# Start-up loads split over two DMA queues, one weighing operation for both planes, regrouped first norm and new orders in a two-layer spectral and MLP kernel

## The chip, the cores and the metric

The kernel runs on one core of one Trainium2 chip. The metric is device time in microseconds (us) of one execution; seven runs of the kernel before gave a median of 354.47 us (353.44 to 354.94). A core has TensorE (PE, its weight loads are PEld), VectorE (DVE), ScalarE (ACT), GpSimd (POOL) and SyncE (SP), each of which takes its instructions in the order in which they are written, and 16 DMA engines that serve all queues.

## The reference, cut to what matters

Two kinds of block alternate, A, B, A, B, on x of 2048 rows by 512, in bf16:

```
x = x + A(layernorm(x));  x = x + B(layernorm(x));  and once more

A(x):  y = irfft2(rfft2(x) * (w_r + i w_i))          # w_r, w_i are 2048 x 257
B(x):  h  = gelu(layernorm(x) @ w1)                  # 512 x 512
       hs = shift(h) @ w2                            # four column groups, shifted by +1, -1, +2, -2 rows
       x1 = x + hs
       return x1 + gelu(layernorm(x1) @ w3) @ w4     # 512 x 1792, 1792 x 512
```

Both pairs of blocks use the same weights.

## The kernel before, in words

Row s of x is kept as partition s // 16 and slot q = s % 16, so a slot is a tile of 128 x 512. The transforms are matmuls with tables made on the host. A pair of blocks is one call of `layer` (L455), and each letter of an order string (ORDER_0 for the start, ORDER_A and ORDER_B for the two calls, L747 to L787) calls one small function with an index; a digit behind a point chooses the PSUM bank, a last letter V or A chooses DVE or ACT. Nothing reorders the instructions afterwards: the order strings are the order on every engine.

The start, `first_front` (L403). For each slot q: `s` takes the sums of the norm (DVE bn_stats L257, or, for slots in ON_ACT, two passes on ACT, L319 and L270), `i` aggregates them on DVE (L286), `f` does the same for the slots of ACT on POOL (L325 to L327), `S` takes the root on ACT (L331) for a group of slots, `J` its reciprocal on DVE (L334), `Q` scales the table T by it (DVE L348, ACT L350), `O` does the matmuls of a pair of slots (L361, L363) with FILL small matmuls on zeros behind it (L243), and `G` copies the result into V (L149 on DVE, L151 on ACT). V holds all slots.

The layer. `d` (L476) multiplies V by the table FA, `t` copies to SBUF (TV), `q` (L500) multiplies by the table TL, `x` copies (X), `p` (`weigh`, L515) multiplies X by the weights W, one DVE operation for the real plane and one for the imaginary one, into PB; `b` (L524) multiplies PB by the table TR, `m` copies into hT. A unit u is one or two of the 16 frequency blocks, and `d`, `t`, `q`, `x`, `p` work by unit. `d` of any block reads all slots of V. `N` (L710) makes a negated copy of half of TR on DVE, which `b` reads. When all `m` are done, `D` (L540), `Y`, `P` (L552) transform back, `a` (L560) adds to x, `s`, `r`, `n` normalise (ACT L270, POOL L276 to L304, DVE L339 or ACT L341), and `T` (L579) transposes by DMA from SP's queue. Then come the MLP matmuls: `v` (L591), `h` its gelu, `u` (L607), `f` and `k`, `o`, `U`, `w` (L642), `g` its gelu, `W` (L655), `A` (L660). At the end of the first layer the start of the second one is mixed in: `B`, `j` (norm sums, L257 and L286), `S` (POOL, L293 and L294), `Q`, `O`, `G`; there `G` of the first five pairs copies the right half on ACT and folds the left half with it on DVE (`fold_V`, L385). `X` puts matmuls on zeros into a named bank. `z` loads the gelu table on ACT (L715), and `L` permutes W on DVE (L704, L705).

Loads (`load_all`, L154). SP's queue carries, in this order, x in eight DMAs, FA, half of TL, and W in 18 DMAs (L208 to L211), with halves of TL and TR between them, then G and Tinv. A DMA on ACT's queue loads T. The DMA of W fills only the even partitions; at the end of `first_front` POOL copies them to the odd ones in four DMAs (L213, one for each quarter of the blocks), each of which waits for its quarter of W, with `turn_TL` (L219, L220) ahead of the first two, which makes the second half of TL from the loaded one. Then `load_mlp` (L187) loads w1 to w4 from SP's queue behind a small DMA that waits for the last copy of W.

Of the kernel before, what the change touches and what calls it, by code (L numbers as in the profile page):

```python
# [16 lines left out]
P = 128  # L17
# [136 lines left out]
def load_all(K, A_x, A_w_r, A_w_i, B_w1, B_w2, B_w3, B_w4):  # L154
# [14 lines left out]
    table("FA", nc.sync)  # L169
    K.TL = K.const.tile([P, NB, 2, P], BF16, name="TL")  # L170
    K.TR = K.const.tile([P, 3, NH, 64], BF16, name="TR")
    load_TL = lambda sl: nc.sync.dma_start(K.TL[:, sl, 0], dram["TL"][:, sl])
    load_TL(slice(0, 8))
    K.W = K.const.tile([P, 2, NH, 257], BF16, name="W")
    K.later = []
    for lo in range(0, NH, 8):
        for pl, w in enumerate((A_w_r, A_w_i)):
            load_W(K, w, pl, lo, lo + 8)
        if lo == 8:
            load_TL(slice(8, 16))  # L180
        if lo in (0, 16):
            nc.sync.dma_start(K.TR[:, 0:2, lo:lo + 16], dram["TR"][:, :, lo:lo + 16])
    for k in ("G", "Tinv"):
        table(k, nc.sync)
    K.load_G2 = lambda: nc.sync.dma_start(K.G[:], dram["G2"])

    def load_mlp():  # L187
        gate2 = K.const.tile([1, 16], BF16, name="gate2")
        nc.sync.dma_start(gate2[:], K.W[1:2, 1, NH - 1, 1:17])
        for k, w, n, c in (("w1", B_w1, 4, D), ("w2", B_w2, 4, D), ("w3", B_w3, 4, FH), ("w4", B_w4, 14, D)):  # L190
            t = K.const.tile([P, n, c], BF16, name=k)
            nc.sync.dma_start(t[:], w.rearrange("(t p) n -> p t n", p=P))
            setattr(K, k, t)
# [8 lines left out]
def load_W(K, w, pl, lo, hi):  # L202


    v = w.rearrange("(m j) f -> m j f", j=64)
    j1 = max(lo, 1)
    fwd, rev = [K.W[2 * sg::4, pl] for sg in range(2)]
    K.nc.sync.dma_start(fwd[:, lo:hi], v[:, lo:hi])  # L208
    K.nc.sync.dma_start(rev[:, j1:hi], v[:, 65 - hi:65 - j1][:, ::-1])
    if lo == 0:  # L210
        K.nc.sync.dma_start(rev[:, 0], v[:, 32])  # L211
    if pl == 1:
        K.later.append(lambda: K.nc.gpsimd.dma_start(K.W[1::2, :, lo:hi], K.W[0::2, :, lo:hi]))  # L213


def turn_TL(K, sl):

    old, new = [K.TL[:, sl, k].rearrange("p b (c h) -> p b c h", h=2) for k in range(2)]
    K.nc.gpsimd.tensor_scalar(new[:, :, :, 0], old[:, :, :, 1], -1.0, None, op0=ALU.mult)  # L219
    K.nc.gpsimd.tensor_copy(new[:, :, :, 1], old[:, :, :, 0])  # L220
# [25 lines left out]
class Stats:  # L246
# [156 lines left out]
def first_front(K):  # L403
# [51 lines left out]
def layer(K, last):  # L455
# [5 lines left out]
    PB = [K.grp.tile([P, 7, 2, 2, 256], BF16, name="PB", tag="gT") for _ in range(2)]  # L461
    n_pab = [0]
# [27 lines left out]
    def over_q(u):  # L490
# [5 lines left out]
        for i, b in enumerate(bs):  # L496
            for t in range(2):
                for h in range(2):
                    r = slice(64 * h, 64 * h + 64)
                    nc.tensor.matmul(o[:, h, i * 256:(i + 1) * 256], lhsT=K.TL[r, b, t],  # L500
                                     rhs=TV[r, i, t * 256:(t + 1) * 256], start=(t == 0), stop=(t == 1))

    def take_q(u, eng):
        X[u] = K.stream.tile([P, 2, 512], BF16, name="X", bufs=2)
        copy(K, X[u][:, :, 0:256 * len(UNITS[u])], ps.pop(("q", u)), eng)

    def weigh(u):
        n = len(UNITS[u])
        x = X.pop(u)[:, :, 0:256 * n].rearrange("p h (n f) -> p h n f", f=256)
        pab[u] = []  # L510
        for pl in range(2):
            t = PB[n_pab[0] % 14 // 7][:, n_pab[0] % 7]
            n_pab[0] += 1
            w = K.W[:, pl, 2 * u:2 * u + 2 * n, 1:257].rearrange("p (n h) f -> p h n f", h=2)
            nc.vector.tensor_tensor(t[:, :, 0:n], x, w, op=ALU.mult)  # L515
# [221 lines left out]
FILL = {0: 4, 1: 3, 2: 3, 3: 3, 4: 3}  # L737
GROUPS = [[0, 2, 3, 4], [7, 8, 9, 10], [11, 12], [14, 15], [1, 5], [6, 13]]
ON_ACT = [1, 5, 6, 13]
FIRST = [[0, 2], [3, 4], [1, 5], [7, 8], [9, 10], [11, 12], [6, 13], [14], [15]]  # L740
# [7 lines left out]
s0 s2 s1 s3 i3 s5 f4 i0 i2 s4 i4 S0 s7 J0 Q0P s6 Q3V Q4V s8 s10 S4 J4 i7 O1 Q2A O0 s9 s13 Q1P i8 f5 i10 i9 Q5V s11 S1  # L748
G1A J1 Q9V Q10V Q8P S5 s12 G0A i11 i12 O2 S2 O4 J5 Q7P s15 J2 G2A s14 i14 i15 Q12V Q11P O3 G4A Q6P S3 G3V O5 Q13A J3
Q15V Q14P O6 G6V G5A O8 G8A O7 G7A  # L750
"""
ORDER_A = """
d1.5 t1V d0.6 t0A d2.2 N0 t2A q1.4 d4.6 x1V p1 d10.4 t10V q0.0 t4A x0A p0 q2.2 x2A d6.6 t6V q4.4 x4A p2 p4 N1 d12.0
q6.6 t12A b1.3 d8.4 x6A p6 m1A q10.0 x10A p10 b3.2 b0.7 t8A b2.6 d14.1 m3A m0V m2A b6.0 q8.4 x8A t14V q12.2 x12A b10.7
m6V b5.1 m5A b4.5 d15.0 t15A b11.2 p8 p12 b9.6 q14.3 m4V m10A q15.0 x14A p14 x15A b7.7 m7A b12.3 m9A b13.1 m12A p15
b14.0 m13A m11V b8.7 m8A m14V b15.5 m15A m15V D1.1 D0.5 z0 L13 Y1V Y0A D3.3 P2.0 a2 Y3A P3.7 a3 s2 P1.6 a1 P0.0 a0
D2.4 s3 Y2V s1 s0 D4.1 Y4A r0 P6.6 a6 s6 P7.3 a7 P5.4 P4.6 a5 P9.3 s7 a4 s5 s4 n2V n3V T1 D5.0 Y5A D7.4 Y7A n0V n1V T0
D6.6 P8.2 a9 a8 P11.5 r1 n7V Y6A s8 P10.0 n4A c1 s9 n6V a11 s11 n5V P14.1 P15.6 a10 T3 a15 s10 P13.4 a13 s15 a14 T2
s13 s14 r2 P12.5 a12 L9 n8V v0.2 n11V n10V s12 r3 v1.0 h1 n9V T4 h0 v3.5 v2.0 h3 u0.7 h2 n12V n15V L14 T5 c0 u2.1 n14A
f2 T7 n13V E2 L11 u3.4 f3 k3 u1.2 f0 v4.0 k0 k2 v5.6 f1 k1 R0 h5 E0 E3 T6 c2 v6.4 v7.2 h4 u5.7 h6 h7 E1 o1V c3 u6.6  # L760
o3V f5 u13.4 u15.0 o0A U0 o2V f6 f13 E6 u10.6 f15 E15 k6 k13 u7.3 f7 k7 u9.7 E7 u4.0 k5 E5 f4 k4 E4 u8.5 f8 U1 f10 k10
R1 w5.2 g5 w0.5 f9 o6V g0 u11.7 w1.0 g1 L7 k9 w2.5 g2 L10 E8 o4A w3.3 g3 k8 w4.1 E13 u12.6 f12 L5 g4 o7V w6.4 U3 E12
E10 g6 W1.0 L1 L12 W2.2 f11 E11 A2 u14.1 f14 E14 k12 o5A k11 E9 U2 w8.4 g8 w9.6 g9 w7.1 g7 w10.6 k14 g10 w11.4 g11
W0.6 R2 o10V k15 R3 w13.4 o9V A0 w12.2 W3.7 g12 g13 o14A W4.4 W7.1 A1 B1 j1 L6 A3 o13V o11A W6.3 A7 B7 B3 j3 A6 o8A B6
U4 U5 w15.1 g15 w17.6 w14.0 g17 g14 w19.6 g19 A4 o15A U7 B0 j0 L4 B2 w16.4 g16 B4 j4 j2 w18.6 g18 w20.4 W5.0 S0 Q1
o12V U6 g20 W8.4 j6 W10.7 w21.1 g21 Q2 A5 B5 A10 L8 A8 W9.6 B10 L2 Q3 L15 A9 w25.4 g25 w23.6 w24.1 j5 L3 g23 B8 O1.3
L0 W11.7 j8 w27.5 j7 S1 G1A G1V A11 w22.3 g27 Q6 j10 Q0 B11 B9 j9 Q7 g24 j11 S2 Q9 g22 w26.0 O3.4 G3A Q4 Q5 Q10 O2.6
G3V G2A g26 W12.3 Q8 A12 G2V B12 j12 W15.5 A15 B15 j15 O0.3 G0A G0V S15 W13.7 A13 B13 j13 W14.2 Q11 O5.5 G5A S12 Q12
S13 Q15 O15.7 A14 B14 j14 S14 Q13 O4.0 G4A G15V O6.3 G6A X4.0 Q14 O14.6 G14A X4.6 G4V G15A X8.2
"""  # L770
ORDER_B = """
d15.3 d1.6 t15A d4.0 t1V q1.2 x1A d8.4 t4V t8A q15.6 x15A p1 q4.2 d12.0 t12A x4V p15 p4 d10.6 t10A b1.3 q12.1 x12V m1A
p12 q8.4 x8A p8 d2.6 t2A d6.0 t6A d14.4 q10.6 x10A q2.2 x2A d0.5 b9.1 m9A t14V t0A p10 b12.6 m12V b4.4 m4A p2 b8.3 m8A
b13.0 q6.1 q0.6 m13A q14.4 x0V x6A p0 b5.3 m5A b15.0 b3.6 m3A b2.1 x14A b11.2 m11A m2A b0.6 p6 b7.7 p14 b10.4 m0A
b14.3 m7V m10A m15V m15A b6.5 m14V m6A D3.6 D2.0 Y2A D1.2 Y1A Y3V P6.4 a6 P4.5 a4 P5.6 s6 a5 s4 s5 P7.4 a7 s7 r1 D0.2
Y0V D5.6 Y5A P2.5 a2 P3.1 a3 P0.0 a0 P1.2 s2 a1 P11.4 s3 s0 s1 D4.5 r0 n5A P10.7 n7V D6.2 n6V Y6A a11 D7.0 s11 Y7A n4V
Y4V T3 P8.5 n0A a10 P13.6 n2V n3V s10 c1 a13 s13 P12.4 n1V a8 P9.2 a9 s8 P14.1 T2 P15.0 a15 v2.6 a12 a14 s9 r2 n9V
n10V T1 h2 n8V s12 s15 s14 r3 v3.2 T0 n11V h3 v1.6 v0.4 c0 h1 n14V h0 T5 u3.7 n13A u2.5 u0.0 f0 u1.1 f1 T4 v5.3 v4.1
n15A n12A f2 k1 E2 f3 E3 h5 u4.0 f4 k0 k3 T6 h4 k2 R0 T7 v6.3 h6 v7.1 h7 k4 E1 o1V u15.3 E4 o2V o3V U1 E0 c3 u13.5 f13
u14.6 f15 o0A u5.0 f14 u8.2 c2 f8 k8 u10.7 u12.6 f12 u9.2 E8 f9 k9 u6.5 f6 k15 E6 f5 E5 f10 u7.1 f7 U0 w4.2 k6 E7 g4  # L780
k7 k10 w0.6 w2.4 g2 u11.1 f11 E11 k13 E10 k5 R1 o4V g0 w5.2 g5 E15 w1.4 k11 w3.2 g1 R2 o6A o7V g3 o5A E9 U3 U2 w6.5 g6
E12 o11A W1.2 A1 W3.1 y1 E13 A3 y3 w12.2 g12 w9.6 o8A g9 w8.2 g8 w10.0 g10 E14 w7.4 g7 w11.2 g11 w13.0 g13 W4.3 o10A
# [35 lines left out]
```

## Time and profile before

| | |
|---|---|
| median of seven runs | 354.47 us |
| the profiled execution: its time, its span | 354.14 us, 352.2 us |
| granted TensorE clock, mean | 0.999 |
| busy share: PE, ACT, DVE, POOL | 97%, 57%, 53%, 20% |
| start, until the first `d` | 0 to 20.90 us |
| first layer: `d` to `b`; `D` to `P`; MLP | to 41.79; to 57.15; to 183.25 us |
| handover to the second layer, until its first `d` | 183.25 to 189.00 us |
| second layer: `d` to `b`; `D` to `P`; MLP | to 208.84; to 224.09; to 348.75 us |
| last addition and store | to 352.2 us |

The span is that of the profiled execution, from its first to its last instruction; about 2 us of its time lie outside of it. A row of a timeline gives start, duration, engine, line, operation, what is written and read, and in brackets the idle time ahead of it and who ended it. A PE that is shown as busy may still be waiting behind the end of its last matmul, which is modelled, so the starts of the matmuls tell more than the busy share.

### The profile page before, as it was taken

What the parts mean: (1) busy time and instruction counts of PE and PEld (TensorE: products, weight loads), DVE (VectorE), ACT (ScalarE), POOL (GpSimd) and SP (SyncE); (2) the same over time, 40 slices, a digit from 0 to 9 for tenths busy, and PEclk for the clock granted to TensorE, in tenths of its full rate; (3) what the DMA queues carried; (4) which work ended last, traced back from release to release, by engine and by line L of the source; (5) the groups of instructions that cost most, each with busy time, mean ns of one, the idle gap of its engine ahead of it and who ended that gap; (6) DMA issues with size and microseconds to landing.
All of it is one profiled execution on the core that took longest, in us unless ns stands there. A gap on an engine that the chain in (4) does not pass through costs nothing.

```text
span 352.2 us, 5586 instructions
## 1 busy us (share of the span) xinstructions
PE 340.9 (97%) x2124; PEld 188.7 (54%) x2124; DVE 184.9 (53%) x442; ACT 200.7 (57%) x355; POOL 68.8 (20%) x171
## 2 busy tenths in 40 slices
PE   8889899999999999999999999999999999999996
PEld 6667785444444444444557888544444444444442
DVE  5869989669270444176576979845732004001003
ACT  5989899585736406213416979976583660442400
POOL 1440037462030101001120004645050010000000
PEclk9999999999999999999999999999999999999999
DMA  7996926611030030300000000763003005101003
GB/s 234 274 331 228 376 72 120 119 36 26 1 61 0 0 61 18 72 0 2 1 2 0 2 2 2 121 106 64 12 7 85 0 0 106 45 0 47 0 30 104
DMA packets 47210, 24.35 MB, mean 69 GB/s; under 512 B 36816, under 2 KB 43984, under 8 KB 47184
## 3 DMA queue, kind: packets, MB, share of 16 engines
q1 hardware_dynamic: 46464, 21.84, 24.8%
q0 software_dynamic: 576, 2.11, 1.5%
q8 instruction: 16, 0.26, 0.3%
q14 instruction: 10, 0.08, 0.1%
q10 hardware_dynamic: 144, 0.07, 0.1%
HBM read 11.41 MB, written 2.10 MB: 38 GB/s over the span
## 4 chain that ended last, share of the span: by engine, by line
PE 79%; ACT 6%; DMA 6%; issue 3%; DVE 3%; SPq 1%; POOL 1%; POOLq 0%; DVEq 0%; ACTq 0%
PE ps L655 27%; PE ps L642 27%; PE ps L591 8%; PE ps L607 8%; ACT hT L151 2%; PE ps L476 2%; DMA xT<-xn 2%; PE ps L540 2%; DVE x_state L560 2%; ACT xn L270 1%; DMA x_state<-in_A_x_dram 1%; PE ps L500 1%; DMA W<-W 1%; DMA W<-in_A_w_i_dram 1%; PE ps L524 1%
## 5 line engine op out<-in xcount | busy, mean ns | idle before, releaser
L649 ACT ACTIVATE gT<-ps 128x1024 bf16<-128x1024 f32 x56 | 56.6, 1024 | 84.1 <-PE ps L642 81.0
L642 PE MATMUL ps<-xT,w 128*128 128x512 bf16 x448 | 99.3, 379 | 0.0
L655 PE MATMUL ps<-w,gT 128*128 128x512 bf16 x448 | 99.0, 379 | 0.0
L660 DVE TENSOR_TENSOR x_state<-ps,x_state 128x512 bf16<-128x512 f32 x32 | 21.5, 689 | 111.7 <-PE ps L655 111.7
L642 PEld LDWEIGHTS <-w 128*128 128x128 bf16 x448 | 43.8, 98 | 52.9
L655 PEld LDWEIGHTS <-gT 128*128 128x128 bf16 x448 | 43.8, 98 | 52.1
L615 DVE SCALAR_TENSOR_TENSOR xn<-xn,ln_c,ps 128x512 bf16<-128x512 bf16 x32 | 23.2, 745 | 18.5 <-PE ps L607 16.1
L270 ACT ACTIVATE junk<-xn 128x512 bf16<-128x512 bf16 x32 | 19.9, 624 | 16.8 <-DVE xn L615 16.8
L591 PE MATMUL ps<-xT,w 128*128 128x512 bf16 x128 | 28.4, 379 | 0.8 <-DMA xT<-xn 0.8
L607 PE MATMUL ps<-w,hT 128*128 128x512 bf16 x128 | 29.1, 379 | 0.0
L276 POOL TENSOR_SCALAR ln_mv<-ln_s 128x4 f32<-128x4 f32 x16 | 5.5, 346 | 91.2 <-DVE x_state L560 52.2
L560 DVE SCALAR_TENSOR_TENSOR x_state<-ps,x_state 128x512 bf16<-128x512 f32 x32 | 20.4, 683 | 2.6 <-PE ps L552 1.9
L515 DVE TENSOR_TENSOR PB<-X,W 128x1024 bf16<-128x1024 bf16 (+1 forms) x40 | 21.0, 581 | 0.1
L591 PEld LDWEIGHTS <-w 128*128 128x128 bf16 x128 | 12.4, 98 | 16.1 <-issue 1.5
L607 PEld LDWEIGHTS <-hT 128*128 128x128 bf16 x128 | 12.5, 98 | 15.1
L257 DVE BATCH_NORM_STATS2 ln_st<-x_state 128x6 f32<-128x512 bf16 x28 | 18.8, 686 | 3.5 <-DMA x_state<-in_A_x_dram 3.2
L270 ACT ACTIVATE xn<-x_state 128x512 bf16<-128x512 bf16 x32 | 19.7, 620 | 0.5 <-DVE x_state L560 0.2
L598 ACT ACTIVATE hT<-ps 128x512 bf16<-128x512 f32 x32 | 17.2, 598 | 1.6 <-PE ps L591 1.5
L540 PE MATMUL ps<-G,hT 128*128 128x256 bf16 x128 | 15.1, 273 | 2.1 <-DVE hT L149 1.2
L476 PE MATMUL ps<-FA,V 128*128 128x256 bf16 x128 | 16.1, 273 | 0.8 <-DMA W<-in_A_w_i_dram 0.8
L552 PE MATMUL ps<-Y,Tinv 128*128 128x256 bf16 x128 | 15.8, 272 | 0.7 <-DVE Y L149 0.5
L293 POOL TENSOR_SCALAR ln_ve<-ln_mv 128x4 f32<-128x4 f32 (+1 forms) x15 | 3.6, 239 | 63.7 <-DVE ln_mv L286 63.0
(78 smaller groups left out, 402.0 us busy)
## 6 DMA issues: line engine op xcount, KB each, us to landing
w<-in_B_w_dram SPq DMA_DIRECT2D x2, 1792.0 KB, 12.3
W<-W POOLq DMA_DIRECT2D x4, 514.0 KB, 4.7
x_state<-in_A_x_dram SPq DMA_DIRECT2D x8, 256.0 KB, 5.4
out_dram<-x_state SPq DMA_DIRECT2D x16, 128.0 KB, 1.9
TR<-tab_TR SPq DMA_DIRECT2D x2, 512.0 KB, 5.3
w<-in_B_w_dram SPq DMA_DIRECT2D x2, 512.0 KB, 4.5
W<-in_A_w_r_dram SPq DMA_DIRECT2D x7, 128.5 KB, 5.0
W<-in_A_w_i_dram SPq DMA_DIRECT2D x7, 128.5 KB, 4.5
```

The lines of the kernel that those rows point to most:

```text
L270: K.nc.scalar.activation(out, src, ACT.Square, bias=0.0, scale=D ** -0.5, accum_out=self.s[:, i, 1:2])
L476: nc.tensor.matmul(oi[:, 1 - h], rhs=K.FA[:, t, h], lhsT=V[:, 2 * t + h, 2 * b:2 * b + 2].rearrange("d b q c -> d (b q c)"), start=(t == 0 ...
L515: nc.vector.tensor_tensor(t[:, :, 0:n], x, w, op=ALU.mult)
L540: nc.tensor.matmul(o[:, i, e * 256:(e + 1) * 256], lhsT=M[:, F, e, 2 * m + i, :], rhs=K.G[:, F, e, :], start=(F == 0 and e == 0), stop=(F ...
L560: nc.vector.scalar_tensor_tensor(K.x[:, q, :], ps.pop(("P", q)), 1.0, K.x[:, q, :], op0=ALU.mult, op1=ALU.add, accum_out=ln[g].s[:, i, 0:1])
L591: nc.tensor.matmul(o[:, i], lhsT=K.w1[:, t, j * P:(j + 1) * P], rhs=xT[g][:, :, t, :], start=(t == 0), stop=(t == 3))
L607: nc.tensor.matmul(o, lhsT=K.hT[:, j, st:st + P], rhs=K.w2[:, j, :], start=(j == 0), stop=(j == 3))
L615: nc.vector.scalar_tensor_tensor(xn[:, q, :], xn[:, q, :], ln[q // 4].c[:, q % 4:q % 4 + 1], ps.pop(("u", n)), op0=ALU.mult, op1=ALU.add, ...
L642: nc.tensor.matmul(o[:, i], lhsT=K.w3[:, c, t * P:(t + 1) * P], rhs=xT3[g][:, :, c, :], start=(c == 0), stop=(c == 3))
L649: nc.scalar.activation(gT[g][:, 2 * j:2 * j + 2, :], ps.pop(("w", k)), ACT.Gelu_apprx_tanh, bias=0.0, scale=1.0)
L655: nc.tensor.matmul(o, lhsT=gT[g][:, t, i * P:(i + 1) * P], rhs=K.w4[:, t, :], start=(t == 0), stop=(t == 13))
L660: nc.vector.tensor_tensor(K.x[:, q, :], ps.pop(("W", n)), K.x[:, q, :], op=ALU.add)
```

## The change

- Loads. ACT's queue now also carries the two small DMAs of W's odd rows (`rev[:, 0]` before), behind T and ahead of ACT's first operation. SP's queue carries x and then only W. FA, TL, TR and the copies of W to the odd partitions go to POOL's queue, in `load_rest`, together with the two `turn_TL`, in the order of the diff; POOL takes it up after its last operation of the start (`f1`). G and Tinv go behind the small DMA that waits for the last copy of W.
- `weigh` is one DVE operation for both planes: X is stored as 2n blocks of 256 and read twice, with a step of zero over the planes, and W and PB are read and written as 2 x 2n x 256. Each of the two PB tiles has three places for units of two blocks and one for a unit of one block, so four units of one block share two places; in the order of the second layer p14 writes the place of unit 15 ahead of b15, which then reads p14's values.
- The first norm has five groups of slots instead of six, in the order of the slots, and ACT takes the sums of slots 1 and 5 alone, not of 1, 5, 6 and 13. `f` works by slot. FILL is 3, 3, 2, 2, 2 instead of 4, 3, 3, 3, 3.
- TL is stored with the two halves apart. `scaled_T` can work on POOL, which no order uses.
- All three orders are new.

```
+    for pl, v in enumerate(planes):
+        nc.scalar.dma_start(K.W[2::4, pl, 0], v[:, 32])
+    for lo in range(0, NH, 8):
+        for pl, v in enumerate(planes):
+            load_W(K, v, pl, lo, lo + 8)
...
+    def load_rest():
+        q = nc.gpsimd
+        load_TL = lambda k: q.dma_start(K.TL[:, 0, 8 * k:8 * k + 8], dram["TL"][:, 8 * k:8 * k + 8])
+        load_TR = lambda k: q.dma_start(K.TR[:, 0:2, 16 * k:16 * k + 16], dram["TR"][:, :, 16 * k:16 * k + 16])
+        double = lambda k: q.dma_start(K.W[1::2, :, 8 * k:8 * k + 8], K.W[0::2, :, 8 * k:8 * k + 8])
+        table("FA", q)
+        load_TL(0)
+        double(0)
+        turn_TL(K, slice(0, 8))
+        load_TL(1)
+        load_TR(0)
+        double(1)
+        turn_TL(K, slice(8, 16))
+        double(2)
+        double(3)
+        load_TR(1)
...
         nc.sync.dma_start(gate2[:], K.W[1:2, 1, NH - 1, 1:17])
+        for k in ("G", "Tinv"):
+            table(k, nc.sync)
...
-        for pl in range(2):
-            t = PB[n_pab[0] % 14 // 7][:, n_pab[0] % 7]
-            n_pab[0] += 1
-            w = K.W[:, pl, 2 * u:2 * u + 2 * n, 1:257].rearrange("p (n h) f -> p h n f", h=2)
-            nc.vector.tensor_tensor(t[:, :, 0:n], x, w, op=ALU.mult)
...
+        k = n_pab[n]
+        n_pab[n] += 1
+        if n == 2:
+            t = PB[k % 2][:, 2 * (k % 6 // 2):2 * (k % 6 // 2) + 2]
+        else:
+            t = PB[k % 2][:, 6].rearrange("p (l h) f -> p l h f", l=2)
+        pab[u] = t
+        nc.vector.tensor_tensor(t, X.pop(u)[:, 0:2 * n].unsqueeze(1).to_broadcast([P, 2, 2 * n, 256]),
+                                K.W[:, :, 2 * u:2 * u + 2 * n, 1:257], op=ALU.mult)
...
-FILL = {0: 4, 1: 3, 2: 3, 3: 3, 4: 3}
-GROUPS = [[0, 2, 3, 4], [7, 8, 9, 10], [11, 12], [14, 15], [1, 5], [6, 13]]
-ON_ACT = [1, 5, 6, 13]
+FILL = {0: 3, 1: 3, 2: 2, 3: 2, 4: 2}
+GROUPS = [[0, 1, 2, 3], [4, 5, 6, 7], [8, 9, 10, 11], [12, 13], [14, 15]]
+ON_ACT = [1, 5]
```

The orders, at the places of which the prediction speaks: the start; the beginning of the first layer; its end; the beginning of the second one.

```
-s0 s2 s1 s3 i3 s5 f4 i0 i2 s4 i4 S0 s7 J0 Q0P s6 Q3V Q4V s8 s10 S4 J4 i7 O1 Q2A O0 s9 s13 Q1P i8 f5 i10 i9 Q5V s11 S1
-G1A J1 Q9V Q10V Q8P S5 s12 G0A i11 i12 O2 S2 O4 J5 Q7P s15 J2 G2A s14 i14 i15 Q12V Q11P O3 G4A Q6P S3 G3V O5 Q13A J3
-Q15V Q14P O6 G6V G5A O8 G8A O7 G7A
+s0 i0 s3 s2 i2 i3 s4 s1 f0 S0 J0 Q2V Q3V O1 i4 Q1V s6 s7 i6 s5 Q0A i7 s11 G1A f1 s9 S1 J1 O0 s8 G0A Q6A s10 i9 Q7A i11
+i8 i10 s13 Q4A O3 s12 Q5A S2 J2 G3A Q8A i13 i12 S3 O2 Q10V Q11V O5 Q9A s15 s14 G2A J3 i15 i14 S4 Q12V G5A Q13V O4 J4
+Q14V Q15V O6 G6A O7 G4V O8 G8A G7V
...
-d1.5 t1V d0.6 t0A d2.2 N0 t2A q1.4 d4.6 x1V p1 d10.4 t10V q0.0 t4A x0A p0 q2.2 x2A d6.6 t6V q4.4 x4A p2 p4 N1 d12.0
+d1.7 t1V d2.0 N0 t2A q1.2 d0.6 t0A x1V p1 d4.4 t4A d10.0 t10V q0.2 x0A q2.6 x2A p0 d6.4 t6V q4.2 x4A d12.0 t12A q10.4
...
-S13 Q15 O15.7 A14 B14 j14 S14 Q13 O4.0 G4A G15V O6.3 G6A X4.0 Q14 O14.6 G14A X4.6 G4V G15A X8.2
+G5A Q15 O15.5 A14 O4.6 G4A G15A B14 j14 S14 Q13 O6.3 X4.0 G6A G15V Q14 O14.0 G14A X8.2 X4.6 G4V
...
-d15.3 d1.6 t15A d4.0 t1V q1.2 x1A d8.4 t4V t8A q15.6 x15A p1 q4.2 d12.0 t12A x4V p15 p4 d10.6 t10A b1.3 q12.1 x12V m1A
+d15.0 t15A d4.4 t4A d1.3 d8.6 t1V q1.0 x1A p1 t8A q4.4 x4V q15.2 x15A p15 d12.0 p4 d10.6 b1.3 t12A q12.4 t10A x12V p12
```

In the first order a letter P behind Q falls to ACT before the change.

## The prediction

> **What bounds the kernel now.** I read the stretches of time first (span, each engine's busy time and count, clock, DMA share, GB/s):
>
> ```profile
> 10.00:15.00 5.00, 4.01 (x34) 3.15 (x33) 4.23 (x16) 5.00 (x15) 3.08 (x6) 1.00 0.96 267
> 35.00:40.00 5.00, 5.00 (x83) 4.55 (x81) 5.00 (x11) 5.00 (x11) 0.00 (x0) 1.00 1.00 379
> 82.00:156.00 74.00, 74.00 (x345) 33.55 (x344) 33.02 (x75) 31.97 (x46) 8.32 (x20) 1.00 0.13 25
> 251.00:330.00 79.00, 79.00 (x367) 35.82 (x366) 14.36 (x33) 39.12 (x56) 7.52 (x18) 1.00 0.14 32
> ```
>
> From 57 to 183 us and from 224 to 349 us PE is never idle, and the change adds and takes no matmul there: new orders can gain nothing in these 251 us, only lose. In the start ACT (fourth time) is full from 10 us on, and the DMA engines too (0.96). In the first part of a layer, `d` to `b`, ACT and DVE are both full.
>
> Then the chain of waits, in order of time, at the handover to the second layer, with DVE's timeline of the same place:
>
> ```profile
> 186.08 1.57 ACT V L151 x2
> 187.65 0.04 issue
> 187.69 1.47 PE ps L243 x12
> 189.16 1.75 PE ps L476 x16
> ```
>
> ```profile
> 186.64 1.42 DVE L385 TENSOR_TENSOR V<-ps,right 128x256 bf16<-128x256 f32 x4 [0.28 <-PE ps L243]
> ```
>
> V is complete at 188.06 (the fold, 186.64 + 1.42), but the first `d` starts at 189.0, behind twelve matmuls on zeros. And the fold waited for PE L243: matmuls on zeros that go to the bank it reads. This wait is about to grow.
>
> Last, POOL's timeline, since the loads move there, and the groups of the weighing operation with one row of it in time:
>
> ```profile
> 12.54 1.66 POOL L219 TENSOR_SCALAR TL<-TL 128x512 bf16<-128x512 bf16 x1
> 14.11 0.77 POOL L220 COPY TL<-TL 128x512 bf16<-128x512 bf16 x1
> 14.79 0.87 POOL L213 DMA_DIRECT2D W<-W  x1
> 20.95 1.65 POOL L219 TENSOR_SCALAR TL<-TL 128x512 bf16<-128x512 bf16 x1 [5.29 <-DMA TL<-tab_TL]
> ```
>
> ```profile
> L515 DVE TENSOR_TENSOR PB<-X,W 128x1024 bf16<-128x1024 bf16 x24 | 15.2, 688 | 0.0
> L515 DVE TENSOR_TENSOR PB<-X,W 128x512 bf16<-128x512 bf16 x16 | 6.0, 420 | 0.1
> ```
>
> ```profile
> 30.82 2.50 DVE L515 TENSOR_TENSOR PB<-X,W 128x1024 bf16<-128x1024 bf16 x4
> ```
>
> In a row, four operations of 1024 take 2.50 us, 0.62 each, and (38.10, four in 1.44) those of 512 take 0.36.
>
> **Part by part.** Differences are after minus before.
>
> 1. *Start, -0.4.* ACT did the sums of four slots (3.87 to 5.20 for one, 1.3 us each) and does two: -2.7. It scales 7 slots, not 9 (0.4 each): -0.8. DVE takes two more bn_stats (0.66) and aggregations (0.1), +1.5, two more scalings (0.25), +0.5, and one of its copies has 512 columns instead of 1024, -0.55. Laying DVE's new order end to end from 3.87, with 0.66, 0.1, 0.17 (reciprocal), 0.25 and 1.2, and holding it only for the arrival of slots 2 to 5 (6.48 in the chain), the last copy ends at 20.0; ACT's end is 20.1. Before it was 20.85. The two small loads on ACT's queue (0.6 each, the rows of L211) push the table load from 1.12 to 2.3; it ends at 3.6, ahead of the first x at 3.87: nothing, 0.2 if not covered. Of the 0.75 only half reaches ACT: its first copy of TV was of one block (21.98) and is now of two, `t2`, behind 12 matmuls of 0.11: 20.1 + 1.3 + 0.2 = 21.6. From there to `D` ACT has the same copies as before (by letters: six `t`, nine `x`, eleven `m`), 18.6 us with 0.7 idle. So `D` comes 0.4 earlier.
>
> 2. *Tables on POOL's queue, 0, up to +3.* `f1` waits for ACT's sums of slot 5 (ends 8.0) and takes 0.7, as L325 to L327 did. FA and half of TL are issued by 10.1 (0.7 each, the rows of L213), the first copy of W by 12.5, when its quarter has landed (13.46 before; its four DMAs now stand right behind x). FA needs 6.5 us to land by its old row, 16 us, and is wanted at 20.1. The critical one is the first half of TR: it stands behind `turn_TL`, which waits for TL. With TL's old 6.9 us, 2.4 for `turn_TL`, 1.4 for two issues and TR's old 5.3, TR lands at 26.1; with T's unloaded 2.8 both times, at 19.5. The bytes wanted by then (x 2.1, W 2.1, FA, TL and TR 1.3, one copy 0.5: 6.0 MB) at the 300 GB/s of the stretches from 2 us on give 22, which I take. `N0` on DVE waits for it, and behind `N0` stand `x1` and `p1`; ACT misses `x1` only when `N0` ends after 23.3 (x1 0.7, `q0` 0.5 and ACT's copy is due at 24.65), that is, TR lands after 22.8. So 0 with a cover of 0.8, +3.0 at 26.1, and no gain from an earlier landing, because ACT bounds the part. The other half of TR (28 to 30) is due at `N1`, 31. G now waits for the last copy of W (27 to 29), lands 4.2 later, and is due at 41. [...]
>
> 3. *One weighing operation, 0 on the path.* From 512 to 1024 an operation grows by 0.26; one of 2048 is 0.62 + 2 x 0.26 = 1.14 against 2 x 0.62, one of 1024 0.62 against 2 x 0.36. Per layer, six and four: 6 x 0.10 + 4 x 0.10 = -1.0 on DVE. ACT covers it: DVE's first-layer part sums to 17.8 from 20.8, ending 38.6, against ACT's 41. The upper bound is the copy from PSUM (L149, 1.22 per 1024): 2.3 and 1.2, +9 per layer on DVE, then 26.7 against 18.6, and `D` 6 later in each layer. The nearest row is L515 itself, with the same W at its odd start, so 1.14. [...]
>
> 4. *`D` to `v`, first layer, +0.3.* The gelu table (1.28) leaves its idle place at 41.3 for the place ahead of the first `h`; there ACT has it done at +17.3 (from `D`), `h1` can start at +17.5: hidden, 1.3 if ACT runs late. DVE's new order reaches `n1`, the last input of the first transposes, at +10.95 (before 52.47 - 41.79 = 10.7), and n6 at +14.75 (before 56.0, +14.3). The transposes follow, so 0.1 of the 0.4 is left at `v`.
>
> 5. *MLP parts, 0.* PE is at its floor; `U1` to the first `w` keeps some 0.4 of cover in the new order. Bound 0 to +1.
>
> 6. *Handover, +0.75.* Up to `O14` the steps after the last `W` are the same (A14, B14, j14, S14, Q14): `O14` starts at 186.41. Then the new order has X8 and X4 and only behind them the fold G4V, and X4.6 writes bank 6, which the fold reads. So 186.41 + 0.44 + 12 x 0.109 + 0.1 = 188.25, fold 1.42, `d` at 189.75 against 189.0.
>
> 7. *Second layer, +0.8.* By letters ACT takes one 1024 `t` (0.95) and one 512 `x` (0.54) more and one `m` (0.54) less, +0.95, DVE gives up 2.1. ACT now has 17.5 us of copies and 1.6 idle, most of it around the first copies; the new order keeps some 1.1 (`x1` waits for `t1` on DVE): 0.65 + 18.4 + 1.1 - 19.8 = +0.35, taken as +0.5 with the half `m` at the end. `D` to `v`: the last input of the transposes at +11.35, before +11.04: +0.3.
>
> Tail: last `W`, addition, store as before.
>
> Sum: -0.4 + 0.3 + 0.75 + 0.8 = +1.45: 354.14 becomes 355.6. The profiled execution lies 0.33 under the median of 354.47, so I forecast **355.8**. About 0.2%, 0.7 us, is what a measurement of this kernel can tell from no change.
>
> **Rivals.**
> - *The gaps of ACT close* (the other side: faster). DVE is lighter by 1.0 in the first layer and 2.1 in the second, so what ACT waits for comes earlier. For it: ACT's copies are 18.6 and 18.4, PE's matmuls of the part only 18.1. Price: the first layer gains its 0.7 of idle and the full 0.75; the second ends at 0.65 + 18.4 + 0.3 - 19.8 = -0.45, and `D` to `v` loses nothing. -1.45 - 0.45 + 0.75 = -1.15, 353.3. It decides when ACT is idle for under 0.4 us between its first TV copy and `D`.
> - *TR is late*, +2 to +3 on top of the sum: 358 to 359. For it: `turn_TL` sat 5.29 us waiting for TL before; against it: SP's weights drain by then.
> [...]
> - *Little of it shows*: the handover costs 0.75 and the start gives it back; 354.5.
>
> **How the numbers follow.** Forecast 0.40, gaps close 0.27, TR late 0.17, little shows 0.12, rate lost 0.04. The low end takes in the closed gaps with 0.7 to spare, 352.6; the high end late TR, 359.0. Slower: most of forecast, TR and rate, 0.56; faster: most of the gaps' case, 0.24; within 0.2%: 0.20.
>
> **What would show it.** First `d` near 20.1; `N0` at 22 to 23, DVE idle ahead of it for TR; the weighing (L527 in the changed file) at 1.2 for 2048; `D` near 41.4; at the handover the fold behind twelve L243 and `d` 0.7 later after the last `W`; second `D` some 20.3 after `d`. Wrong if PE idles in an MLP part, or if `D` moves by more than 1.

## The result, and the profile after

The changed kernel takes **355.82 us** (median of 22 runs, 354.21 to 358.18) against 354.01 us before (56 runs, 353.05 to 354.96): ratio 1.005, 95% interval 1.0039 to 1.0061. It is slower by 1.8 us, and the forecast was 355.8. As the points below show, that number came out in part by luck, because errors of opposite sign cancelled. Nine of the 22 executions have a mean granted TensorE clock of 0.989 to 0.995 and a median of 356.37; the other thirteen (0.998 to 1.000) have one of 354.98; run 1 has the profile of one execution with such a clock, 0.50 in one stretch of it.

The profiled execution took 355.86 us with a span of 354.1. I cut both spans at the same landmarks, which are starts of matmuls. The third row has the kernel in which the two waits found below are gone (the experiment e4_both).

| us | start to first `d` | `d` to `D` | `D` to `v` | `v` to last W | last W to second `d` | `d` to `D` | `D` to `v` | `v` to the end | span |
|---|---|---|---|---|---|---|---|---|---|
| before | 20.90 | 20.89 | 15.36 | 126.10 | 5.75 | 19.84 | 15.25 | 128.11 | 352.2 |
| after | 19.59 | 23.24 | 15.24 | 126.28 | 6.10 | 20.46 | 14.85 | 128.34 | 354.1 |
| e4_both | 18.76 | 21.47 | 14.84 | 126.26 | 5.33 | 19.87 | 14.74 | 128.33 | 349.6 |

Two cells of the row after stand out: `d` to `D` of the first layer, +2.35, and the handover with the part behind it, +0.35 and +0.62.

The stretches of the kernel after (span, then the busy time and count of PE, PEld, DVE, ACT and POOL, granted clock, DMA share, GB/s) first show what has not changed, the MLP part of the first layer, and then the place of the first loss, with the same three microseconds of the kernel before below it:

```profile
82.00:156.00 74.00, 73.98 (x343) 33.40 (x342) 34.05 (x82) 34.56 (x50) 9.59 (x20) 1.00 0.18 28
```

```profile
23.00:26.00 3.00, 1.12 (x15) 0.77 (x14) 2.05 (x3) 1.22 (x2) 3.00 (x5) 1.00 0.45 184
```

```profile
23.00:26.00 3.00, 3.00 (x35) 2.28 (x32) 2.42 (x4) 3.00 (x4) 1.70 (x3) 1.00 1.04 362
```

From 23 to 26 us PE works for 1.12 us of 3 and ACT for 1.22; before, both were full there (3.00 and 3.00). The DMA engines aren't full either (0.45, where the kernel before has 1.04). The chain of waits of the kernel after, in order of time (start, duration, what), names what is waited for:

```profile
18.02 5.86 DMA TR<-tab_TR
...
23.91 0.04 DVE TR L722
...
24.85 0.68 DVE X L149
25.53 0.05 issue
25.57 0.83 PE ps L509 x12
```

L722 is `N0`. On DVE, `x1` (24.85) stands behind it, and PE's next matmuls on TV (25.57) behind `x1`. DVE's timeline gives the idle time (first the kernel after, then the kernel before, where `N0` waits for nothing), and POOL's shows why TR was asked for only at 18.02:

```profile
23.91 1.01 DVE L722 TENSOR_SCALAR TR<-TR 128x1024 bf16<-128x1024 bf16 x1 [2.96 <-DMA TR<-tab_TR]
```

```profile
22.24 0.64 DVE L710 TENSOR_SCALAR TR<-TR 128x1024 bf16<-128x1024 bf16 x1
```

```profile
14.14 0.62 POOL L183 DMA_DIRECT2D W<-W  x1 [4.16 <-DMA W<-in_A_w_i_dram]
15.13 1.66 POOL L228 TENSOR_SCALAR TL<-TL 128x512 bf16<-128x512 bf16 x1 [0.37 <-DMA TL<-tab_TL]
16.72 0.76 POOL L229 COPY TL<-TL 128x512 bf16<-128x512 bf16 x1
17.41 0.61 POOL L181 DMA_DIRECT2D TL<-tab_TL  x1
18.02 0.73 POOL L182 DMA_DIRECT2D TR<-tab_TR  x1
...
22.34 1.63 POOL L228 TENSOR_SCALAR TL<-TL 128x512 bf16<-128x512 bf16 x1 [2.96 <-DMA TL<-tab_TL]
...
25.86 0.73 POOL L182 DMA_DIRECT2D TR<-tab_TR  x1
```

The load of TR waits in POOL's order behind a copy of W, which itself waited 4.16 us for its quarter of W, and behind `turn_TL` (2.4 us with its copy). In the kernel before, SP issued it at 10.97. From issue to landing it took 5.86 us, hardly more than the 5.3 of the kernel before (median of its two halves): TR was late because it was asked for late.

The second place, in the chain and in DVE's timeline of the kernel after:

```profile
187.26 0.42 DVE V L149
187.68 0.21 DVE Tq L358
...
188.53 1.32 PE ps L252 x12
...
189.88 1.43 DVE V L395 x4
191.30 0.05 issue
191.35 1.70 PE ps L485 x14
```

```profile
189.88 1.42 DVE L395 TENSOR_TENSOR V<-ps,right 128x256 bf16<-128x256 f32 x4 [2.00 <-PE ps L252]
```

DVE is free at 187.88 and the fold waits 2.00 us for twelve matmuls on zeros, four of which go to the bank that it reads.

These four do more than hold the fold up. `X4.6` writes its zeros over the left half of the first of `O4`'s two slots ahead of the fold, which then takes zeros for it; in the kernel before `X4.0` does the same, as `O4` has bank 0 there. Both kernels leave that half of one slot out of the second layer. Where an expectation below calls V of `O4`'s pair "the computed one", no zeros are written there.

And the weighing, as groups of shapes of the kernel after (busy us, mean ns, idle time ahead):

```profile
L527 DVE TENSOR_TENSOR PB<-X,W 128x2048 bf16<-128x2048 bf16 x12 | 14.4, 1224 | 0.1
L527 DVE TENSOR_TENSOR PB<-X,W 128x1024 bf16<-128x1024 bf16 x8 | 5.5, 691 | 1.4 <-ACT X L151 1.3
```

### The profile page after: what moved, and what is told of

The parts are those of the page before. It is cut to its first block, busy times and chain, and to the rows that moved or that the text cites. A ratio compares the mean times of both kernels' runs of the same rounds, so it can differ in the third digit from the quotient of the medians.

```text
span 354.1 us, 5547 instructions
## 1 busy us (share of the span) xinstructions
PE 339.9 (96%) x2120; PEld 188.0 (53%) x2120; DVE 183.8 (52%) x431; ACT 197.0 (56%) x340; POOL 71.9 (20%) x176
## 4 chain that ended last, share of the span: by engine, by line
PE 83%; DMA 5%; ACT 5%; DVE 4%; issue 1%; POOL 1%; DVEq 0%; POOLq 0%; ACTq 0%
PE ps L654 27%; PE ps L667 27%; PE ps L603 8%; PE ps L619 8%; PE ps L552 3%; PE ps L485 3%; PE ps L564 2%; PE ps L509 2%; ACT hT L151 2%; DMA TR<-tab_TR 2%; DMA TL<-tab_TL 2%; PE ps L536 2%; ACT X L151 1%; DMA x_state<-in_A_x_dram 1%; DMA xT<-xn 1%
## 5 line engine op out<-in xcount | busy, mean ns | idle before, releaser
L610 ACT ACTIVATE hT<-ps 128x512 bf16<-128x512 f32 x32 | 18.1, 597 | 8.7 <-PE ps L603 8.6
L266 DVE BATCH_NORM_STATS2 ln_st<-x_state 128x6 f32<-128x512 bf16 x30 | 19.9, 682 | 4.1 <-DMA x_state<-in_A_x_dram 3.8
L619 PEld LDWEIGHTS <-hT 128*128 128x128 bf16 x128 | 12.5, 98 | 15.1
L527 DVE TENSOR_TENSOR PB<-X,W 128x2048 bf16<-128x2048 bf16 (+1 forms) x20 | 19.6, 1011 | 1.5 <-ACT X L151 1.3
L151 ACT ACTIVATE X<-ps 128x1024 bf16<-128x1024 f32 (+1 forms) x17 | 14.4, 885 | 3.2 <-PE ps L509 2.5
```

What stands on the lines that cost most here:

```text
L151: K.nc.scalar.activation(dst, src, ACT.Copy, bias=0.0, scale=1.0)
L619: nc.tensor.matmul(o, lhsT=K.hT[:, j, st:st + P], rhs=K.w2[:, j, :], start=(j == 0), stop=(j == 3))
```

## The experiments

My theory after the result: the loss is two waits, `N0` for TR and the fold for the matmuls on zeros, less what the start gained. The rival: the new orders cost it inside the layers, or the loads on POOL's queue do so as a whole. Each kernel was timed against the kernel before on the same chip; "before" was 353.77, 353.96 and 354.14 us in the three groups (runs 1 to 4, 5 to 8, 9 to 12). A difference between kernels of different groups carries these 0.2 to 0.4 us.

**1. The fold without its wait (e1_fill_bank).**

```
-... X8.2 X4.6 G4V
+... X8.2 X4.2 G4V
```

> The changed kernel with the last four matmuls on zeros of the handover sent to bank 2 instead of bank 6, which the fold G4V reads. In this kernel no zeros are written over the left half of O4's result ahead of its fold, so V of that pair of slots is the computed one. Theory (the loss is two waits: N0 for TR in the first layer, and the fold behind twelve matmuls on zeros at the handover): the fold no longer waits 2.00 us for PE but starts when O4 and G4's right half are there and DVE is free; the first `d` of the second layer comes at the end of the twelve matmuls or of the fold, 0.8 to 1.2 us earlier from the last W, and the time falls from 355.8 to about 354.8. Rival (the new orders and the weighing cost it inside the layers): the first `d` waits for another thing as long, and the time stays within 0.3 of 355.8.

Measured: 354.13 us (353.18 to 355.86), ratio to before 1.0011 (0.9993 to 1.0028). DVE's and then PE's timeline of this kernel:

```profile
187.86 0.42 DVE L149 CAST V<-ps 128x256 bf16<-128x256 f32 x1 [0.90 <-ACT V L151]
188.20 0.28 DVE L358 TENSOR_SCALAR Tq<-T,ln_r 128x256 bf16<-128x256 bf16 x1
188.39 1.41 DVE L395 TENSOR_TENSOR V<-ps,right 128x256 bf16<-128x256 f32 x4
```

```profile
188.96 1.47 PE L252 MATMUL ps<-zeros 128*128 128x256 bf16 x12
190.27 2.46 PE L485 MATMUL ps<-FA,V 128*128 128x256 bf16 x21
```

The fold runs right behind DVE's other work, with no bracket. From the last W to `d` it is 5.32 us instead of 6.10, and `d` to `D` 19.88 instead of 20.46: 1.36 in all, because in the kernel after the first 24 `d` also took 3.37 us instead of 2.78, while the rest of the fold came in. I had counted only the first part. The rival said 0.3 at most, and falls for this place.

This profiled execution (355.04 us, mean granted clock 0.994) shows one thing more. Its first layer's `d` to `D` took 25.02 us, longer than the 23.24 of the kernel after, although `N0` came at the same time (24.05): the first `d` was earlier (18.45), so PE idled longer. PE's timeline, first of the kernel after, then of this one, and a stretch of this one:

```profile
25.57 0.83 PE L509 MATMUL ps<-TV,TL 64*128 64x256 bf16 x12 [1.88 <-DVE X L149]
```

```profile
25.25 1.46 PE L509 MATMUL ps<-TV,TL 64*128 64x256 bf16 x12 [2.70 <-DVE X L149]
26.64 1.89 PE L485 MATMUL ps<-FA,V 128*128 128x256 bf16 x8
```

```profile
25.50:28.00 2.50, 2.50 (x19) 1.53 (x16) 2.20 (x3) 1.62 (x2) 0.86 (x2) 0.50 0.86 322
```

Behind 1.88 us of idling the granted clock stayed at 1.00. Behind 2.70 us it was 0.50 from 25.5 to 28.0, and the same twelve `q` took 1.46 instead of 0.83, eight `d` 1.89 instead of 1.05: 1.5 us on top of the wait. Four of the twelve executions of run 1 have a mean clock of 0.994 or 0.995; the median of the other eight is 353.60, 1.4 below the 354.98 of the kernel after with its clock kept, so the fold's 1.36 is found there too. That the nine executions of the kernel after with such a mean lost it at this place is likely but not shown, as none of them was profiled; and a low mean alone doesn't make an execution long, for three of the kernel before with 0.994 and 0.995 took 354.23 to 354.73.

**2. `N0` behind `t6V` (e2_n0_late).**

```
-d1.7 t1V d2.0 N0 t2A ... x2A p0 d6.4 t6V q4.2
+d1.7 t1V d2.0 t2A ... x2A p0 d6.4 t6V N0 q4.2
```

> The changed kernel with N0 moved in DVE's order from ahead of x1 to behind t6V, so that x1, p1, t10V, p0 and t6V no longer stand behind its wait for TR (23.9 us). Theory: PE's idle 1.88 us at 25.6 and ACT's 1.79 at 26.0 go, `d` to `D` of the first layer falls from 23.2 to about 21.0 to 21.4, and the time from 355.8 to about 353.8. If TR is late for the first b as well (its reader b2.7), at most 0.5 of it comes back. Rival: ACT, which has as many copies as before, is the bound of the part and N0's wait was beside it; the time falls by less than 0.5.

Measured: 353.14 us (352.69 to 353.82, and one of 356.98), ratio 0.9991 (0.9970 to 1.0011): 2.7 below the kernel after, and 1.9 below it where only executions that kept their clock are compared (353.07 and 354.98). DVE's timeline of this kernel, over the same stretch:

```profile
20.26 0.69 DVE L149 CAST X<-ps 128x512 bf16<-128x512 f32 x1 [0.56 <-PE ps L509]
20.98 0.69 DVE L527 TENSOR_TENSOR PB<-X,W 128x1024 bf16<-128x1024 bf16 x1
...
25.66 0.54 DVE L722 TENSOR_SCALAR TR<-TR 128x1024 bf16<-128x1024 bf16 x1
```

`x1` starts at 20.26 instead of 24.85, and `N0`, at 25.66, waits for nothing. TR was asked for at 17.62, hardly earlier than in the kernel after; what moved is its reader. But for one of twelve (356.98, mean clock 0.993) the executions also lie within 1.2 us, those of the kernel after within 4.

**3. TR's load earlier on POOL's queue (e3_tr_early).** `load_TR(0)` moves from behind `load_TL(1)` to ahead of `double(0)`.

> The changed kernel with the load of TR's first half issued on POOL's queue ahead of the first copy of W, at about 10 us instead of 18.0. Theory: at 5.9 us from issue to landing TR is there at 16 to 18, N0 does not wait, and the time falls by about 2, to 353.8, as if N0 were moved; N0 takes 0.43 to 1.0 us. What may eat some of it: 512 KB come 8 us earlier into the stretch in which the DMA engines are full with x and W, so W's first quarter, its copy, and p1 come later; each us of that which DVE or ACT sees costs as much. Rival (the loads on POOL's queue as a whole take what the change loses): the first `d` or p1 comes later by as much as N0 comes earlier, and the time stays within 0.5 of 355.8.

Measured: 355.39 us (353.58 to 357.65), ratio 1.0051 (1.0024 to 1.0078). The median is that of the rival, the profiled run (354.04) that of the theory. In it, `N0` doesn't wait, but the next table does, a little:

```profile
20.71 0.41 DVE L722 TENSOR_SCALAR TR<-TR 128x1024 bf16<-128x1024 bf16 x1
...
31.70 0.43 DVE L722 TENSOR_SCALAR TR<-TR 128x1024 bf16<-128x1024 bf16 x1 [0.67 <-DMA TR<-tab_TR]
```

The copy of W was issued at 15.06 and the second half of TR at 26.55, both later than in the kernel after (14.14, 25.86). What the longer executions waited for isn't in this profile. The four longest (356.14 to 357.65) have a mean granted clock of 0.994 or 0.995, the other six (353.58 to 355.52) 0.997 to 1.000, so in those four PE may have idled as long as in the profiles of runs 1 and 10 (2.70 and 3.91 us), which is not shown; run 10 shows such a wait for a near relation.

**4. Both (e4_both).** The edits of 1 and 2.

> The first two changes together: N0 behind t6V, and the last four matmuls on zeros to bank 2. As in the first, V of O4's pair of slots is the computed one. Theory: the two waits are in different parts and add up, 355.8 - 2.0 - 0.9 = about 352.9, some 1.1 faster than the kernel before; this is then what the earlier start, the lighter weighing and the new orders are worth without the two waits. Rival: it stays at or above the kernel before (354.0), and the new orders themselves cost time.

Measured: 352.20 us (351.41 to 352.31, and one of 357.10), ratio 0.9951 (0.9933 to 0.9969). Less the two waits, the change is faster than the kernel before by 1.6 us (353.77 in this group); the fold's part of it, against run 2, is 0.94. The execution of 357.10 has a mean clock of 0.990.

**5. The kernel before with fewer matmuls on zeros (e5_before_fill).** `X4.6` and `X8.2` go from its handover.

> The kernel before without the twelve last matmuls on zeros of its handover (X4.6 and X8.2). Theory: in the kernel before, V was complete at 188.06 and the first `d` stood behind these twelve at 189.0; without them `d` comes 0.7 to 0.9 after... that is, 0.7 to 0.9 earlier, and the time falls from 354.0 to about 353.2. The twelve are then what the handover already paid before the change. Rival: without them PE gets a lower granted clock for the first matmuls behind the gap, and the time stays at 354.0 or grows.

Measured: 352.96 us (351.99 to 353.73), ratio 0.9969 (0.9956 to 0.9982). PE's timeline there:

```profile
188.24 1.92 PE L476 MATMUL ps<-FA,V 128*128 128x256 bf16 x16 [0.96 <-ACT V L151]
```

From the last W to `d` it is 4.73 us instead of 5.75; the sixteen `d` run at their usual pace (1.92 us, as in the first layer), the granted clock is 1.0, and the parts behind are the same to 0.1 (19.85, 15.30). So these matmuls kept nothing up here that the run shows; they cost 1.0 in the kernel before too.

**6. Two weighing operations (e6_two_ops),** in the kernel of run 4.

```
-        nc.vector.tensor_tensor(t, X.pop(u)[...].to_broadcast([P, 2, 2 * n, 256]), K.W[:, :, ...], op=ALU.mult)
+        x = X.pop(u)[:, 0:2 * n]
+        for pl in range(2):
+            nc.vector.tensor_tensor(t[:, pl], x, K.W[:, pl, ...], op=ALU.mult)
```

> The kernel with N0 late and the last four matmuls on zeros to bank 2 (352.2), with the weighing split again into one operation for each plane, in the same layout. As there, V of O4's pair of slots is the computed one. Theory (one operation saves 0.10 per pair of operations, beside ACT, which bounds the part): DVE is busier by about 1.0 in each layer, and the time grows by 0 to 0.5. Rival (the lighter DVE is what makes this kernel faster than the one before): the time grows by 1 to 2. A time below 352.2 would say that the large operation holds something up.

Measured: 352.25 us (351.75 to 353.56), ratio 0.9956 (0.9939 to 0.9973), against 352.20 for run 4: nothing that can be told apart. In the second layer, where no load disturbs, `d` to `D` is 20.11 instead of 19.87. The profiled execution is the longest of the eight (353.56); in its first layer `N1` waited 1.39 us for TR, so its 23.10 from `d` to `D` says nothing of the weighing.

**7 and 8. New start with old orders, old start with new orders.** e7_old_orders_n0 is the changed kernel with the three order strings' layers (ORDER_A, ORDER_B) taken from the kernel before and `N0` behind `t6V`; e8_new_orders is the kernel before with ORDER_A and ORDER_B of the changed one.

> The changed kernel with its start, loads and one weighing operation, but the orders of the two layers from the kernel before, with N0 behind t6V there too. Theory (new orders gain nothing but for N0's place and the handover): as the kernel with N0 late, 353.1, less the handover's difference of 0.35 and what the second layer's first part has longer (0.6): about 352.3. Rival (the new orders gain in the layers): 354 or more. Rival the other way (the new orders lose): under 351.8.

> The kernel before (its start, its loads on SP's queue, two weighing operations) with the orders of the two layers of the changed one. TR lands there at 16.3, so N0 does not wait. Theory: the handover has the fold behind twelve matmuls on zeros, +0.35 to the first half of `d` and +0.6 in the part behind it; the rest is as before: about 354.6 to 355.0. Rival (the new orders' inner sequence costs more, as PB and ACT then wait): 355.5 or more. If they gain: under 354.0.

Measured: 354.58 us (353.92 to 356.70), ratio 1.0020 (1.0004 to 1.0036), and 355.78 us (355.49 to 356.42), ratio 1.0052 (1.0035 to 1.0068). My theory fell in both, and the times are those that the rivals named. In the first, DVE's timeline shows a wait that I hadn't thought of, `N1` for the second half of TR:

```profile
31.03 0.43 DVE L722 TENSOR_SCALAR TR<-TR 128x1024 bf16<-128x1024 bf16 x1 [1.80 <-DMA TR<-tab_TR]
```

The old order has `N1` earlier than the new one, and the new loads bring its half later (issued at 25.86; at 18.85 in the kernel before). In the second kernel `N0` and `N1` don't wait, and still the first layer's `d` to `D` is 21.74 instead of 20.89 and the second layer's 20.70 instead of 19.84 (0.59 of that behind the fold: 24 `d` in 3.37 there too, instead of 2.78). Half of the first 0.85 is ACT's first copy of TV, which starts 1.52 behind the first `d` (22.54 and 21.02) instead of 1.08. So with the old start the new orders cost 1.8, and the old orders don't suit the new loads.

**9 and 11. What is left at the handover, and `N1` later.** e9_less_fill is run 4 without `X4.2`; e11_best is that with `N1` moved as well.

```
-... p6 t8A N1 b0.3 ... m3V t15V q12.1
+... p6 t8A b0.3 ... m3V t15V N1 q12.1
```

> The kernel with N0 late (352.2) without the last four matmuls on zeros of its handover, which had gone to bank 2. As there, V of O4's pair of slots is the computed one. Theory: in that kernel V was complete at 186.19 (fold) and 186.15 (ACT's half of O14), and the first `d` stood behind the matmuls on zeros at 186.66; without four of them (0.109 each) it comes at about 186.25, and the time falls by 0.4, to 351.8. Rival (the twelve keep PE's clock up for what follows): the granted clock or `d` to `D` gets worse, and the time stays at 352.2.

> The kernel of the shorter handover (N0 late, four matmuls on zeros less) with N1, the negation of TR's second half, also moved later on DVE, from behind t8A to behind t15V, ahead of the first matmul that reads it. V of O4's pair is the computed one. Theory: in three of five profiles with this load order N1 waited 0.36 to 1.39 for TR's second half at 30.2 to 32.2 us; moved past p10 and t15V it waits no more, so the slower executions go and the median falls by 0.2 to 0.5, to about 351.4; the spread becomes less than 1. Rival: the waits of N1 lay beside ACT, and nothing changes, 351.8.

Measured: 351.61 us (350.83 to 352.02, and two of 355.23 and 356.41), ratio 0.9935 (0.9915 to 0.9955), and 351.39 us (350.76 to 352.38), ratio 0.9921 (0.9904 to 0.9937). The first is as expected: from the last W to `d` it is 4.88 instead of 5.33, and `d` now starts at 187.03, right at the end of the fold (185.59 + 1.41):

```profile
185.59 1.41 DVE L395 TENSOR_TENSOR V<-ps,right 128x256 bf16<-128x256 f32 x4
```

The second is inconclusive. `N1`, at 33.69, waits for nothing, but the five executions spread over 1.6 us, not under 1, and in the profiled one, the longest of them, ACT waited 1.2 us for DVE's PB, which a move of a DVE operation may well have caused; 0.2 us between five runs and twelve isn't told apart. The two long executions of run 9 have a mean clock of 0.995 and 0.994. These two are the fastest kernels of the study, 2.5 and 2.8 us faster than the kernel before.

**10. TR's first half on SP's queue (e10_tr_sp),** `N0` at its place in the change.

```
+        if lo == 0:
+            nc.sync.dma_start(K.TR[:, 0:2, 0:16], dram["TR"][:, :, 0:16])
...
-        load_TR(0)
```

> The changed kernel with N0 where the change has it, but with the load of TR's first half on SP's queue behind the first quarter of W, as in the kernel before, instead of POOL's. Theory (what made TR late is its place behind a copy of W and turn_TL on the engine that issues it, not the bandwidth): issued at 8 to 9 us, it lands before 17, N0 does not wait, the first layer's `d` to `D` is 21.5 to 22 and the time about 353.3 to 353.8; as SP issues the other three quarters of W 0.6 later and POOL one load less, W's copies move little, and the runs lie closer together than those of the changed kernel (354.2 to 358.2). Rival (DMA bandwidth until 24 us is the limit, whoever issues): W's first copy comes later by what TR takes, as in the kernel with TR early on POOL's queue, the runs spread over 4 us again, and the median is 355 or more.

Measured: **357.73 us** (354.18 to 358.61), ratio 1.0088 (1.0056 to 1.0120), the slowest of all. Half of the theory held: `N0` runs at 19.93 without a wait. But POOL's and DVE's timelines show what it did to the rest of the chain:

```profile
17.07 1.66 POOL L229 TENSOR_SCALAR TL<-TL 128x512 bf16<-128x512 bf16 x1 [3.17 <-DMA TL<-tab_TL]
...
27.36 0.74 POOL L184 DMA_DIRECT2D TR<-tab_TR  x1
```

```profile
34.08 0.43 DVE L723 TENSOR_SCALAR TR<-TR 128x1024 bf16<-128x1024 bf16 x1 [3.88 <-DMA TR<-tab_TR]
```

With 512 KB more ahead of it, TL's first half reached POOL at 17.07 instead of 15.13. Everything behind it on POOL came later, the second half of TR too (27.36 instead of 25.86), and now `N1` waits 3.88 us. PE idles behind it, and its granted clock falls as in run 1. PE's timeline and a stretch of it:

```profile
36.30 3.44 PE L537 MATMUL ps<-TR,PB 128*128 128x128 bf16 x32 [3.91 <-DVE hT L149]
```

```profile
36.50:39.00 2.50, 2.50 (x26) 2.50 (x25) 2.50 (x4) 1.06 (x3) 0.00 (x0) 0.50 0.90 277
```

The 32 `b` take 3.44 us instead of 1.95 (at 29.02 in the same profile), so the wait costs 1.5 us more than its length; four of the six executions have a mean clock of 0.994 or 0.995. As I read it, bandwidth and order on the queue are both at work: the bytes that one table asks for earlier delay the next, and POOL's order passes the delay on.

**12. Old orders, `N0` and `N1` late (e12_old_orders_n01).** As run 7, with `N1` behind `t14V`.

> The changed kernel's start, loads and one weighing operation with the orders of the layers from the kernel before, with N0 behind t6V and N1 behind t14V. It tells what the kernel with old orders and N0 late (354.6, slower than expected) lost: there N1 waited 1.80 for TR's second half. Theory (that wait was the loss): 1 to 1.5 faster, 353.1 to 353.6, and the new orders by themselves are then worth nothing beyond it. Rival (the new orders suit the new loads in other places, the copies of W and PB): it stays at 354 or more.

Measured: 353.67 us (352.89 to 354.62), ratio 0.9990 (0.9978 to 1.0001): 0.9 below run 7 (1.1, each against the kernel before of its group), just outside the theory's range. So `N1`'s wait was less than half of the 2.3 by which run 7 missed its 352.3. Against run 11 (351.39) it is 2.3 slower. In their profiles 0.85 of that is the handover (5.73 and 4.88; run 11 has four matmuls on zeros less and another order), 0.6 and 0.4 are the parts `D` to `v` (15.74 and 15.29 against 15.15 and 14.88). So the new orders are worth something there. Run 11's profiled execution was the longest of its five, so the spans differ by 1.3 only, and the rest of the 2.3 I can't assign.

## Why the prediction was right, and where it was wrong

The time was right, and the mechanism of the handover too. The other mechanism of the loss stood among the rivals ("TR is late") and not in the sum, and by its own sign ("if `D` moves by more than 1") the prediction was wrong about the first layer: `D` came at 42.83, 1.04 later than before, where the prediction had it 0.4 earlier. That 355.8 came out all the same was in part luck. By its steps, after minus before:

1. *Start, -0.4: too small.* The first `d` came at 19.59, in the eleven profiles with the new start between 18.34 and 19.59, and not at 20.1. Laying rows end to end was the error: a row's duration runs on into the next operation. In DVE's timeline of the kernel after, one bn_stats takes 0.69, but the operation behind two of them starts 1.17 to 1.29 after the first, where I took 2 x 0.66; behind two scalings it starts 0.37 and 0.39 after the first (at 14.03 and 6.99), where I took 2 x 0.25. Over the 14 bn_stats and nine scalings that is, as an estimate, over 1 us. In the five profiles with the new start and new orders in which neither `N0` nor the other half of TR held DVE for more than 0.7 us (runs 2, 3, 4, 9 and 11), `D` starts at 40.16 to 41.29, that is 0.5 to 1.6 earlier than before.

2. *Tables on POOL's queue, 0: the step that failed.* The estimate that TR lands at 22 was mis-sized; it landed at 23.9. I had derived it from bytes at 300 GB/s; what the profile shows in its place is POOL's order: the first copy of W waited for its quarter until 14.14 where I had 12.5, `turn_TL` followed, TR was issued at 18.02 and took 5.86. By the step's own rule, a wait begins when TR lands after 22.8; the start was earlier than I said by 0.5 as well, and `N0` took 1.01. The price is the 2.7 us of run 2: 1.9 where the clock is kept, the rest probably the clock, which was 0.50 behind 2.70 us of idling in run 1 and 1.00 behind 1.88 in the kernel after, a term that the prediction lacks. That no gain was to be had from an earlier landing was right for `N0` alone; in runs 3 and 10 the next table then came later, and `N1` waited for it, 0.67 and 3.88 us.

3. *Weighing, 0 on the path: right.* 1.22 for 2048 against 1.14 forecast, and run 6 finds nothing. The bound of 2.3 was far off. A lost rate, which has 0.04 among the chances, is shown by no run: 2048 took 1224 ns in the kernel after, and 1024 took 691 there and 688 before.

4. *`D` to `v`, +0.3: no such loss.* -0.12 in the kernel after; 14.84 to 15.24 in all profiles with the new orders, against 14.65 to 15.74 in the four with the old ones. The gelu table load was hidden, as said.

5. *MLP parts, 0: right within its bound.* They are up to 0.2 longer with the new order of the first layer (126.11 to 126.28, against 126.10 and 126.11).

6. *Handover, +0.75: right.* The fold waited for twelve L252 as described; it cost 0.35 up to `d` and 0.59 behind it, where I had all of it ahead of `d`. Run 1 takes it away.

7. *Second layer, +0.8: wrong.* Without the fold's hold, `d` to `D` is 19.87 to 19.88, as before (19.84), and `D` to `v` is 0.4 shorter. ACT's longer list of copies cost nothing that shows.

So -0.4 + 0 + 0.3 + 0 + 0.75 + 0.8 should have read, in the two profiles: -1.31 for the start, +2.35 for `d` to `D` with TR late, -0.12, +0.18 for the MLP, +0.35 and +0.62 for the handover and the part behind it, -0.40, and +0.23 at the end, together +1.9. A TR that costs nothing and a second layer that costs 0.8, a small gain of the start and a loss in `D` to `v` made the same sum. The rival *The gaps of ACT close* had -0.45 for the second layer, and -0.4 came, but in `D` to `v`, where it had nothing, and not in `d` to `D`. By its own condition it fell in the first layer: there ACT was idle 1.79 us at 26.0, behind `x1`. With that wait gone (run 2) the time is 353.14, close to this rival's 353.3.

What stays open: what the long executions of the kernel after and of run 3 waited for, and whether their clock fell behind that wait (only argued from the profiles of runs 1 and 10); and how the 0.85 that the new orders cost in the first layer of run 8 divides beyond ACT's first copy (in run 4, without the two waits, `d` to `D` is still 0.58 longer than before).

## What to carry to other kernels

When a load moves to a queue of an engine that also computes, write down that engine's whole sequence, its waits included, up to the load; here the bytes at 300 GB/s gave 22 for TR's landing, and with POOL's order it came at 23.9. If the load is then late, move its reader back in the reader's order before moving the load forward: run 2 gained 2.7 us by that, run 10 lost 1.9. And look at every filler for the bank that it writes: here matmuls that only fill a gap became a wait of 2.00 us for the fold, which reads their bank, and overwrote what it was to read. Last, look at the granted clock behind a wait of PE: in the profiles of runs 1 and 10 it was 0.50 there, and the wait cost 1.5 us more than its length.

## What the runs showed of the hardware that was not expected

The weighing and `N0` took longer on DVE where they began while POOL worked on `turn_TL`. In the kernel of run 4, DVE's and POOL's timelines:

```profile
21.40 1.00 DVE L527 TENSOR_TENSOR PB<-X,W 128x1024 bf16<-128x1024 bf16 x1
...
24.17 0.68 DVE L527 TENSOR_TENSOR PB<-X,W 128x1024 bf16<-128x1024 bf16 x1
```

```profile
21.25 1.64 POOL L228 TENSOR_SCALAR TL<-TL 128x512 bf16<-128x512 bf16 x1 [2.73 <-DMA TL<-tab_TL]
```

The same weighing takes 1.00 beside it and 0.68 later; in run 11 one took 1.12 (24.61, with POOL at L229 from 24.49), and `N0` in the kernel after 1.01, against 0.40 to 0.43 with POOL idle. In these cases POOL's operation had begun first; in run 12 the weighing did (21.68, POOL's at 21.83), and there it took its 0.69 and POOL's operation 2.05 instead of 1.64. In run 4 the weighing ended at 22.40, half a microsecond before POOL's operation did (22.89; POOL's spans are rough), so by these rows it lost 0.3 and was not held until that operation ended. Why either is slower beside the other, the rows don't show.
